# Shared 4 KB places for raw weights and raw x, and another order of score copies, in a gated mix of Fourier mixing and SwiGLU on one Trainium2 core

## The chip, the cores and the metric

The kernel runs on 1 core of one Trainium2 chip. The metric is the device time of one execution in microseconds (us). The time before is 725.82 us, the median of 3 runs (725.61 to 725.87).

## The reference, cut to what matters

For x of 2048 tokens by 512, all in float32:

```python
g = sigmoid((x * gate_w).sum(-1, keepdims=True))
a = dft_seq_re @ (x @ dft_hid_re.T) - dft_seq_im @ (x @ dft_hid_im.T)   # real part of the Fourier mix
b = (silu(x @ w1) * (x @ w3)) @ w2                                       # SwiGLU, inner width F = 1376
out = g * a + (1 - g) * b
```

## The kernel before, in words

**Products.** Every large product is done on blocks of 2 x 2 with seven products in place of eight (forms B11, B21, B22 and sums T1 to T4 of one side, and sums of the same kind of the other side). Each float32 operand is split into a rounded high part, made by ScalarE (`high`, L108, the activation at L109), and a remainder, made by VectorE (`low`, L111, the subtraction at L112). Each product then takes three matmuls (`mm3`, L118 and L120): high with high, high with low, low with high. A matmul has 128 x 128 stationary and 128 x 512 moving operands.

**Stage 1, gate and up (to about 220 us of the profile).** `ITEMS` lists 22 items (c, g): a chunk c of 128 of the F columns for the half g of the tokens (1024). Item 0 is done by `plain`; `gate_up(n)` does items 1 to 21. An item has seven products of six matmuls: X (five of them, one after another in one PSUM bank; `bank(n % 4)`), Y and Z. `first1` and `first2` of item n + LOOK (LOOK = 3) are done inside item n. The order inside an item is: X with form 4 and its read (L353), Z with form 5 and its read (L356), the next items' `first1`, X with form 3 and an addition on VectorE (L364), Z with form 2 and VectorE's L369 and L370, `first2` with an addition (L289), a copy of the score if there is one, and a Silu (L291), and last X with form 6 and the second half's Silu (L382), which frees the bank for the X of item n + 4, and VectorE's L383.

Raw weights of gate and up come in tiles `ws` of 128 x 1024 float32, 4 KB a partition, in a pool of their own with LOOK + 1 = 4 buffers (`load_w`). They are used for forms `wa` (rounded in the same item) and `wb` (sums `wu` on VectorE, then split). For the first 9 chunks `wb` is stored to DRAM and read back for the second half of the tokens (`load_wb`, L227).

The last chunk has 96 columns of F, and gate_w in the 32 that are left, so rows 96 to 127 of its bank are the scores of the output gate. `put_score(n, j, gate)` copies these 32 rows for the tokens' half j into a tile `sc`: for j = 0 on ScalarE from `s1`, for j = 1 on VectorE from the bank itself, ahead of the Silu of L382. Two small DMAs take them to `gs` in DRAM. It happens for items 11 and 12.

**Stage 2 (from about 220 us).** `STEPS` lists the work of eight blocks. Blocks F (four) multiply the sequence DFT (`cc`) with forms A1 and A2 of x; each has 7 forms x 4 quarters q = 28 steps of 12 matmuls. Blocks H (two) multiply what `hsp` holds of silu(gate) * up with forms of w2. Blocks Y (two) apply the hidden DFT to the F blocks' results, add H's and write out. In the order of a block: P1 (steps 0 to 3, form B11), P5 (4 to 7, T1), P6 (8 to 11, T2), P3 (12 to 15, B22), P7 (16 to 19, T3), P2 (20 to 23, B21), P4 (24 to 27, T4).

Every step ends with `advance(m)`: it issues loads of raw operands (`load_c`, on SP's queue), does a sum on VectorE (`sum_c`) for step m + 4, and splits the operand of step m + 3 (`split_c`) into one of four places `zo`. In the first block T3 is made by a DMA of POOL's queue that adds B12 to B22 in place (L651).

**Places.** `F4` is a list of 4 KB places (`wide` takes the first, `free` appends). In stage 1 it has 4 places (`f4_0` to `f4_3`, pool `f4_a`); when the pools of stage 1 are closed, 9 more are put ahead of them (`f4_4` to `f4_12`, pool `f4_b`), in memory that stage 1 used. Raw w2, raw x for the first forms (A1, `load_a`), the score tile and all raw operands of stage 2 take their places there. `load_c(0)` and `load_c(1)` are called at the ends of items 19 and 20, all else after stage 1.

**Around the first block.** `load_score(0)` reads the scores of the first half from `gs`, spread to all partitions, into a tile of the pool `ut`; it is issued right after stage 1, ahead of the loads of `advance(-1)`. `gates(0)` (ahead of step 2) does the sigmoid and stores g and 1 - g, up to signs, to DRAM; `load_gate` reads them back at step 8. The second forms A2 of x are made from x once more: `load_a2(p)` reads raw x (eight tiles of 128 x 1024) into one of two tiles of `ut` in turn (tags `u3`, `c21`), two ahead of step 4 and each later one when `make_a2(p - 2)` has been issued; `make_a2(p)` is issued ahead of step 8 + p and does one subtraction (L169) and two splits.

Each engine and each queue works in the order of the program, and waits there for semaphores. SP's queue carries nearly all loads, POOL's the stores to DRAM and the adding loads.

Of the kernel before, what the change touches and what calls it, by code (L numbers as in the profile page):

```python
# [7 lines left out]
F32 = mybir.dt.float32  # L8
F32R = mybir.dt.float32r
AF = mybir.ActivationFunctionType  # L10
ALU = mybir.AluOpType

P = 128
S = 2048
D = 512
F = 1376
# [5 lines left out]
NG = NST // 2  # L22
# [3 lines left out]
LOOK = 3  # L26
# [6 lines left out]
def fnet_swiglu_gate_kernel(  # L33
# [20 lines left out]
    nc = tc.nc  # L54

    def pool(name, bufs, side, space=None):
        kw = {} if space is None else {"space": space}
        cm = tc.tile_pool(name=name, bufs=bufs, side=side, reuse_waits="tile", **kw)
        return cm, cm.__enter__()
# [8 lines left out]
    zo_a_cm, zo_a = pool("zo_a", 1, "left")  # L68
    xo0_cm, xo0 = pool("xo0", 1, "left")
    f4_a_cm, f4_a = pool("f4_a", 1, "right")  # L70
    ws_cm, wsp = pool("ws", LOOK + 1, "right")
    wu_cm, wup = pool("wu", 1, "right")
    s1_cm, s1p = pool("s1", LOOK + 1, "right")
    wa_cm, wap = pool("wa", LOOK + 1, "right")
    wb_cm, wbp = pool("wb", 2, "right")
    u4_cm, u4p = pool("u4", 1, "right")
    h_cm, hp = pool("h", 2, "right")
    xo1_cm, xo1 = pool("xo1", 1, "right")
    gate_pools = (ws_cm, wu_cm, s1_cm, wa_cm, wb_cm, u4_cm, h_cm, xo1_cm)

    def bank(k, name):
        return psum.tile([P, 512], F32, tag=f"ps{k}", name=name)
# [3 lines left out]
    F4 = [(f4_a, f"f4_{k}") for k in range(4)]  # L86
# [10 lines left out]
    def wide(name):  # L97
        return take(F4, [P, 1024], F32, name)
# [4 lines left out]
    def free(*tiles):  # L103
        for t in tiles:
            _, places, at = HELD.pop(id(t))
            places.append(at)
# [28 lines left out]
    def flat(ap):  # L135
        return ap.rearrange("p a n -> p (a n)")
# [29 lines left out]
    def forms2(r, t2):  # L166

        r = r.rearrange("p (a n) -> p a n", a=4)
        nc.vector.tensor_sub(r[:, 0], r[:, 1], r[:, 0])  # L169
        split(flat(t2[:, 0, 0:2]), flat(t2[:, 1, 0:2]), flat(r[:, 2:4]))  # L170
        split(t2[:, 0, 2], t2[:, 1, 2], r[:, 0])
# [8 lines left out]
    NI = len(ITEMS)  # L180
# [22 lines left out]
    def sum_xo(g, k, t):  # L203
        ST[g, k] = t
        nc.vector.tensor_sub(t, *(ST[g, v] for v in SUMS[k]))  # L205
# [5 lines left out]
    def split_xo(g, k):  # L211
        split(*xo_parts(g, k))

    WS, WA, WB = {}, {}, {}
# [3 lines left out]

    def load_w(w, lo=0, hi=4):
        if lo == 0:  # L220
            WS[w] = wsp.tile([P, 4, 256], F32, tag="ws", name=f"ws{w}")
        nc.sync.dma_start(WS[w][:, lo:hi].rearrange("p a n -> p (a n)"),
                          w13[SETS[w], :, lo * 256 : hi * 256])

# [41 lines left out]
    def prod(ps, n, wi, xi, start, chain=False):  # L266
        w = WSET[n]
        w, wi = (WA[w], wi) if wi < 3 else (WB[w], wi - 3)
        x = XO[ITEMS[n][1]]
        for q in range(2):  # L270
            sl = slice(q * P, (q + 1) * P)
            mm3(ps, w[:, 0, wi, sl], w[:, 1, wi, sl], x[:, 0, xi, q, :], x[:, 1, xi, q, :],
                start and q == 0, q == 1, chain)
# [10 lines left out]
    def first2(n):  # L284

        y = bank(4 + n % 2, f"Y{n}")
        prod(y, n, 1, 1, True)
        s1 = G[n][1]
        nc.vector.tensor_add(s1, s1, y)  # L289
        put_score(n, 0, s1)  # L290
        nc.scalar.activation(s1, s1, AF.Silu)  # L291

    SC = {}

    def put_score(n, j, gate):


        c, g = ITEMS[n]
        if c < NC - 1:
            return  # L300
        if not SC:
            SC[0] = wide("sc")
        p = F % P - 32 * g
        t = SC[0].rearrange("p (b n) -> p b n", b=2)
        if j == 0:
            nc.scalar.activation(t[p : p + 32, j], gate[F % P :], AF.Copy)
        else:
            nc.vector.tensor_copy(t[p : p + 32, j], gate[F % P :])
        if j == 1:
            nc.gpsimd.dma_start(gs[2 * g : 2 * g + 2].rearrange("b o n -> o b n"), t[p : p + 1])  # L310
            if g == 1:
                at_end.setdefault(n + 1, []).append(lambda: free(SC[0]))
# [16 lines left out]
    def gate_up(n):  # L329
        last = NI - 1  # L330
        x, s1 = G.pop(n)
        z = bank(6 + n % 2, f"Z{n}")
        if n == last - 1:

            u2, g1 = (s1p.tile([P, 512], F32, tag="s1", name=f"{k}_{n}") for k in ("u2", "g1"))
        else:
            h = hp.tile([P, 1024], F32, tag="h", name=f"h{n}")
            u2, g1 = h[:, :512], h[:, 512:]
        u4 = u4p.tile([P, 512], F32, tag="u4", name=f"u4_{n}")
        nw = WSET[n + 1] if n < last else 0  # L340
        if nw in WB or nw == 0:
            nw = None
        elif back(nw):
            load_wb(nw)
            nw = None
        wa = WSET[n + LOOK + 1] if n + LOOK < last else 0
        if wa in WA or wa == 0:
            wa = None
        else:
            load_w(wa, 0, 3 if back(wa) else 4)  # L350

        prod(x, n, 4, 4, False, True)
        nc.scalar.activation(u2, x, AF.Copy)  # L353
        run(early, n)
        prod(z, n, 5, 5, True, True)
        nc.scalar.activation(u4, z, AF.Copy)  # L356
        if nw is not None:
            sums_wb(nw)
        if n + LOOK <= last:
            first1(n + LOOK)  # L360
        if nw is not None:
            high_wb(nw)
        prod(x, n, 3, 3, False, True)
        nc.vector.tensor_add(u4, u4, x)  # L364
        if nw is not None:
            low_wb(nw)
        run(mid, n)
        prod(z, n, 2, 6, False, True)
        nc.vector.tensor_add(u2, u2, z)  # L369
        nc.vector.tensor_mul(u2, s1, u2)  # L370
        store_h(n, 0, u2)
        if wa is not None:
            WA[wa] = wap.tile([P, 2, 3, 256], F32R, tag="wa", name=f"wa{wa}")
            parts_a = wa_parts(wa, 0, 3)
            high(parts_a[0], parts_a[2])
        if n + LOOK <= last:
            first2(n + LOOK)
        if wa is not None:
            low(*parts_a)
        prod(x, n, 6, 2, False, True)  # L380
        put_score(n, 1, x)
        nc.scalar.activation(g1, x, AF.Silu)  # L382
        nc.vector.tensor_mul(g1, g1, u4)  # L383
        store_h(n, 1, g1)
        run(at_end, n)
# [75 lines left out]
    prep_wa(1)  # L461
    first1(1)
    first2(1)
    sum_xo(0, "T1", hp.tile([P, 1024], F32, tag="h", name="t1"))
    sum_xo(0, "T2", ST[0, "B11"])
    prep_wa(2)
    first1(2)
    first2(2)
    split_xo(0, "T2")
    prep_wb(1)  # L470
    sum_xo(0, "T3", ST[0, "B12"])
# [1 line left out]
    prep_wa(3)  # L473
    first1(3)
    first2(3)
    split_xo(0, "T1")
    prep_wa(4)
    sum_xo(0, "T4", ST[0, "B21"])
# [3 lines left out]
    def do(work, n, f, *a):  # L482
        work.setdefault(n, []).append(lambda: f(*a))
# [64 lines left out]
    for n in range(NI):  # L548
# [6 lines left out]
        if n in A1_AT:  # L555
# [2 lines left out]
            do(early, n, lambda p=p: sums1_here(XR[p]))  # L558
            do(mid, n, high_a, p)
            do(early, n + 1, low_a, p)  # L560
    do(at_end, NI - 3, lambda: load_c(0))
    do(at_end, NI - 2, load_a, NG - 1)
    do(at_end, NI - 2, lambda: load_c(1))
    do(early, NI - 1, lambda: sums1_here(XR[NG - 1]))
    do(mid, NI - 1, lambda: split_c(0))
    do(at_end, NI - 1, lambda: split_c(1))
# [87 lines left out]
    def load_c(m):  # L654
        while LOADS and LOADS[0][0] <= m and F4:
            _, blk, k, q = LOADS.pop(0)
            r = RAW[blk, k, q] = wide(f"{k}_{blk}_{q}")
            n = cols(blk, q, k)
            nc.sync.dma_start(r[:, :n], block(blk, k, q)[:, :n])

    def advance(m):
        load_c(m + LEAD + AHEAD)
        sum_c(m + LEAD + 1)
        split_c(m + LEAD)
# [10 lines left out]
    f4_b_cm, f4_b = pool("f4_b", 1, "right")  # L675
    a2_cm, a2 = pool("a2", 1, "right")
    ut_cm, ut = pool("ut", 1, "right")
    F4[:0] = [(f4_b, f"f4_{k}") for k in range(4, 13)]
    ZO[:0] = [(zo_b, f"zo_{k}") for k in range(2, 4)]
    def load_a2(p):  # L680

        XR[p] = flat(ut.tile([P, 2, 512], F32, tag=("u3", "c21")[p % 2], name=f"xs{p}"))
        nc.sync.dma_start(XR[p], xn[p])

    def make_a2(p):
        A2.append(a2.tile([P, 2, 3, 256], F32R, tag=f"a2_{p}", name=f"a2_{p}"))
        forms2(XR.pop(p), A2[p])
        if p + 2 < NG:
            load_a2(p + 2)

    GATES = {}

    def load_score(g):
        t, ng = GATES[g] = [flat(ut.tile([P, 2, 512], F32, tag=k, name=f"{k}g{g}"))
                            for k in ("p5", "u2")]
        nc.sync.dma_start(t.rearrange("p (b n) -> p b n", b=2),
                          gs[2 * g : 2 * g + 2].rearrange("b o n -> o b n").to_broadcast([P, 2, 512]))

    load_score(0)
    high_a(NG - 1)  # L700
    low_a(NG - 1)
    advance(-1)

    def gates(g):

# [168 lines left out]
    def at(blk, n, f, *a):  # L874
        todo.setdefault(START[blk] + n, []).append((f, a))

    at(0, 4, load_a2, 0)
    at(0, 4, load_a2, 1)
    at(1, 1, load_score, 1)
    for p in range(NG):  # L880
        at(0, 8 + p, make_a2, p)
    at(0, 2, gates, 0)
    at(1, 3, gates, 1)
    late = [(w2, w2sp, p) for p in range(len(W2_AT), NP2)] + [(dd, dsp, p) for p in range(KD)]
    for i, (src, sp, p) in enumerate(late):
# [86 lines left out]
```

## Time and profile before

| | |
|---|---|
| median of 3 runs | 725.82 us (725.61 to 725.87) |
| profiled execution, its own time | 725.82 us |
| its span, first to last instruction | 724.0 us |
| TensorE, matmuls | 712.1 us busy (98%), 3089 matmuls |
| TensorE, weight loads | 582.2 us (80%) |
| VectorE | 603.3 us (83%), 731 instructions |
| ScalarE | 368.0 us (51%), 475 instructions |
| GpSimd | 67.6 us (9%) |
| mean granted clock of TensorE | 0.990 |
| DMA | 174.64 MB, mean 241 GB/s |

The engines are named PE (matmuls of TensorE), PEld (its weight loads), DVE (VectorE), ACT (ScalarE), POOL (GpSimd) and SPq (SP's queue of DMAs). Times in the profile are counted from the first instruction of the profiled execution. The busy share is a mean over stages; where an engine ends the wait of another, the waits and the chain of waits tell.

### The profile page before, as it was taken

To read this page: it belongs to the slowest core of one execution; us is meant where nothing else is said; L and a number is where in the kernel's file an instruction comes from. 1 tells how busy PE (TensorE), PEld (TensorE's weight loads), DVE (VectorE), ACT (ScalarE), POOL (GpSimd) and SP (SyncE) were. 2 spreads that over 40 slices of the span, in tenths; PEclk is the share of its full clock that TensorE was granted. 3 is DMA by queue.
4 is the path that set the end of the run, shared out by engine and by line. 5 is a ranking of instruction groups with operands and counts; after the bars stand their busy time and mean duration, and the time that the engine had idled before them with its cause. 6 is when DMAs were issued, how large, how long until landed. Compare 5 with 4: busy or idle time off the path is not lost.

```text
span 724.0 us, 8583 instructions
## 1 busy us (share of the span) xinstructions
PE 712.1 (98%) x3089; PEld 582.2 (80%) x3089; DVE 603.3 (83%) x731; ACT 368.0 (51%) x475; POOL 67.6 (9%) x122
## 2 busy tenths in 40 slices
PE   9999999999998999999999999999999999999997
PEld 6888888788886877888888888888888888888886
DVE  6988888887676968895999699987998797797985
ACT  6565465455444645455536444554545545445451
POOL 0011111121010010000011001100110010010000
PEclk9999999999998998999999999999999999999999
DMA  7575556589887499832289127915799962763932
GB/s 275 202 282 214 198 191 258 200 293 349 329 318 277 196 247 340 294 156 86 69 323 371 42 84 273 399 69 204 306 421 418 395 240 108 291 244 151 331 118 87
DMA packets 45979, 174.64 MB, mean 241 GB/s; under 512 B 5360, under 2 KB 5488, under 8 KB 42096
## 3 DMA queue, kind: packets, MB, share of 16 engines
q1 hardware_dynamic: 32464, 118.50, 44.6%
q0 software_dynamic: 13184, 55.07, 20.1%
q8 instruction: 24, 0.39, 0.2%
q10 hardware_dynamic: 288, 0.52, 0.2%
q14 instruction: 19, 0.16, 0.1%
HBM read 116.92 MB, written 57.16 MB: 240 GB/s over the span
## 4 chain that ended last, share of the span: by engine, by line
PE 88%; DVE 5%; DMA 3%; ACT 2%; issue 1%; SPq 0%; ACTq 0%; DVEq 0%
PE P L120 62%; PE X L120 14%; PE Z L120 7%; PE Y L120 4%; DVE zo L112 2%; DMA xs<-xn 1%; DMA B<-cc 1%; PE C L120 1%; DVE B L634 1%; ACT zo L109 1%; DMA xs_B<-xt 1%; DVE xo L112 0%; ACT h L382 0%; DVE xs_B L205 0%; ACT wb L109 0%
## 5 line engine op out<-in xcount | busy, mean ns | idle before, releaser
L120 PE MATMUL P<-zo,a 128*128 128x512 f32 x1344 | 312.4, 395 | 5.4 <-ACT zo L109 4.3
L120 PEld LDWEIGHTS P<-zo,a 128*128 128x128 f32 x1344 | 255.6, 191 | 62.0 <-ACT zo L109 5.1
L109 ACT ACTIVATE zo<-B 128x1024 fp32r<-128x1024 f32 (+1 forms) x182 | 189.1, 1044 | 184.3 <-PE P L120 95.3
L112 DVE TENSOR_TENSOR zo<-B,zo 128x1024 fp32r<-128x1024 f32 (+1 forms) x182 | 217.4, 1202 | 54.9 <-ACT zo L109 54.3
L120 PE MATMUL P<-zo,H 128*128 128x512 f32 x468 | 106.2, 389 | 0.0
L120 PEld LDWEIGHTS P<-zo,H 128*128 128x128 f32 x468 | 87.9, 188 | 18.2
L634 DVE TENSOR_TENSOR B<-B,B 128x1024 f32<-128x1024 f32 (+1 forms) x78 | 92.7, 1189 | 1.7 <-DMA B<-cc 1.6
L120 PE MATMUL X<-xo,wb 128*128 128x512 f32 x378 | 92.8, 389 | 0.0
L120 PEld LDWEIGHTS X<-xo,wb 128*128 128x128 f32 x378 | 70.9, 188 | 15.0 <-DVE u L364 0.3
L120 PE MATMUL P<-zo,Y 128*128 128x512 f32 x336 | 76.3, 389 | 0.0
L120 PEld LDWEIGHTS P<-zo,Y 128*128 128x128 f32 x336 | 63.1, 188 | 13.1
L319 POOL DMA_DIRECT2D hsp<-h x42 | 23.0, 548 | 127.6 <-DVE h L370 70.4
L120 PE MATMUL X<-xo,wa 128*128 128x512 f32 x126 | 32.6, 391 | 1.4 <-ACT h L382 1.4
L120 PE MATMUL Z<-xo,wa 128*128 128x512 f32 x126 | 32.3, 390 | 0.0
L120 PE MATMUL Y<-xo,wa 128*128 128x512 f32 x126 | 32.1, 389 | 0.0
L120 PE MATMUL Z<-xo,wb 128*128 128x512 f32 x126 | 32.1, 389 | 0.0
L120 PEld LDWEIGHTS X<-xo,wa 128*128 128x128 f32 x126 | 23.5, 188 | 7.1 <-ACT h L382 2.3
L847 ACT ACTIVATE zu<-P 128x512 f32<-128x512 f32 x32 | 19.0, 597 | 19.5 <-PE P L120 19.5
L120 PEld LDWEIGHTS Z<-xo,wa 128*128 128x128 f32 x126 | 23.6, 188 | 5.3 <-DVE xo L112 0.4
L120 PEld LDWEIGHTS Y<-xo,wa 128*128 128x128 f32 x126 | 23.6, 188 | 4.9
L120 PEld LDWEIGHTS Z<-xo,wb 128*128 128x128 f32 x126 | 23.6, 188 | 4.9
L637 DVE TENSOR_TENSOR B<-B,B 128x1024 f32<-128x1024 f32 x22 | 26.8, 1218 | 0.0
(134 smaller groups left out, 546.0 us busy)
## 6 DMA issues: line engine op xcount, KB each, us to landing
B<-cc SPq DMA_DIRECT2D x64, 512.0 KB, 7.0
hsp<-h POOLq DMA_DIRECT2D x42, 256.0 KB, 3.7
B<-hsp SPq DMA_DIRECT2D x20, 512.0 KB, 10.4
wbsp<-wb POOLq DMA_DIRECT2D x8, 1024.0 KB, 4.4
wb<-wbsp SPq DMA_DIRECT2D x8, 1024.0 KB, 6.3
B<-zsp SPq DMA_DIRECT2D x16, 512.0 KB, 8.1
H<-w2sp SPq DMA_DIRECT2D x6, 1024.0 KB, 9.3
ws<-w SPq DMA_DIRECT2D x11, 512.0 KB, 6.8
```

The lines of the kernel that those rows point to most:

```text
L109: nc.scalar.activation(hi, src, AF.Copy)
L112: nc.vector.tensor_sub(lo, src, hi.bitcast(F32))
L120: nc.tensor.matmul(ps, u, v, start=first and n == 0, stop=last and n == 2, skip_group_check=chain)
L319: nc.gpsimd.dma_start(hsp[g, b + k, j // 2, :, j % 2 * 512 : (j % 2 + 1) * 512], h)
L634: nc.vector.tensor_add(t, t, RAW[blk, b, q][:, :n])
L637: nc.vector.tensor_sub(t, RAW[blk, "B12", q], t)
L847: nc.scalar.activation(U[name][:, r], ps[r], AF.Copy)
```

## The change

Raw gate/up weights no longer have a pool of their own: `load_w` takes four further tags of `f4_a`, `f4_4` to `f4_7`, in turn. At the end of item 17 these four join `F4`, and the pool made after stage 1 has only `f4_8` to `f4_12`; there are 13 places as before. `load_c(0)` to `load_c(4)` are called at the ends of items 17 to 21.

Raw x for the second forms takes places from `F4`; `load_a2(p)` is issued ahead of step 4 + p, and `make_a2(p)`, at its old step, frees the place.

The second Silu of an item on ScalarE comes ahead of the score's copy, and the copy is on ScalarE for both halves. The Silu of the first half (`gate1`) leaves `first2` and comes behind both; ahead of item 1 it follows `first2` as before.

`load_score(0)` comes behind `advance(-1)`, and `gates(0)` ahead of step 4 in place of step 2.

On TensorE and on POOL's queue the order of instructions is the same as before. VectorE has two copies fewer and ScalarE two more.

```diff
@@ pools
-    ws_cm, wsp = pool("ws", LOOK + 1, "right")
...
@@ load_w
-            WS[w] = wsp.tile([P, 4, 256], F32, tag="ws", name=f"ws{w}")
+            WS[w] = f4_a.tile([P, 4, 256], F32, tag=f"f4_{4 + w % (LOOK + 1)}", name=f"ws{w}")
@@ first2
         put_score(n, 0, s1)
-        nc.scalar.activation(s1, s1, AF.Silu)
+
+    def gate1(n):
+        nc.scalar.activation(G[n][1], G[n][1], AF.Silu)
@@ put_score
-        if j == 0:
-            nc.scalar.activation(t[p : p + 32, j], gate[F % P :], AF.Copy)
-        else:
-            nc.vector.tensor_copy(t[p : p + 32, j], gate[F % P :])
+        nc.scalar.activation(t[p : p + 32, j], gate[F % P :], AF.Copy)
@@ gate_up
         prod(x, n, 6, 2, False, True)
+        nc.scalar.activation(g1, x, AF.Silu)
         put_score(n, 1, x)
-        nc.scalar.activation(g1, x, AF.Silu)
+        if n + LOOK <= last:
+            gate1(n + LOOK)
@@ loads of the first block, ends of items
-    do(at_end, NI - 3, lambda: load_c(0))
+    n = NI - 1 - LOOK
+    do(at_end, n - 1, F4.extend, [(f4_a, f"f4_{k}") for k in range(4, 5 + LOOK)])
+    for k in range(LOOK + 2):
+        do(at_end, n - 1 + k, lambda k=k: load_c(k))
     do(at_end, NI - 2, load_a, NG - 1)
-    do(at_end, NI - 2, lambda: load_c(1))
@@ after stage 1
-    F4[:0] = [(f4_b, f"f4_{k}") for k in range(4, 13)]
+    F4[:0] = [(f4_b, f"f4_{k}") for k in range(5 + LOOK, 13)]
@@ load_a2, make_a2
-        XR[p] = flat(ut.tile([P, 2, 512], F32, tag=("u3", "c21")[p % 2], name=f"xs{p}"))
+        XR[p] = wide(f"xs{p}")
         nc.sync.dma_start(XR[p], xn[p])
...
-        forms2(XR.pop(p), A2[p])
-        if p + 2 < NG:
-            load_a2(p + 2)
+        forms2(XR[p], A2[p])
+        free(XR.pop(p))
...
-    load_score(0)
     high_a(NG - 1)
     low_a(NG - 1)
     advance(-1)
+    load_score(0)
@@ steps
-    at(0, 4, load_a2, 0)
-    at(0, 4, load_a2, 1)
     at(1, 1, load_score, 1)
     for p in range(NG):
+        at(0, 4 + p, load_a2, p)
         at(0, 8 + p, make_a2, p)
-    at(0, 2, gates, 0)
+    at(0, 4, gates, 0)
     at(1, 3, gates, 1)
```

More of the change, by code (lines that the diff above doesn't have):

```diff
@@ L78, in fnet_swiglu_gate_kernel @@
     xo1_cm, xo1 = pool("xo1", 1, "right")
-    gate_pools = (ws_cm, wu_cm, s1_cm, wa_cm, wb_cm, u4_cm, h_cm, xo1_cm)
+    gate_pools = (wu_cm, s1_cm, wa_cm, wb_cm, u4_cm, h_cm, xo1_cm)
     def bank(k, name):
@@ L463, in fnet_swiglu_gate_kernel @@
     first2(1)
+    gate1(1)
     sum_xo(0, "T1", hp.tile([P, 1024], F32, tag="h", name="t1"))
@@ L468, in fnet_swiglu_gate_kernel @@
     first2(2)
+    gate1(2)
     split_xo(0, "T2")
@@ L475, in fnet_swiglu_gate_kernel @@
     first2(3)
+    gate1(3)
     split_xo(0, "T1")
```

## The prediction

> **What bounds the kernel now.** I read the page first, then the waits of TensorE, its timeline, the windows around its gaps, and the chain of waits there. The page's busy times and the granted clock by slices:
>
> ```profile
> PE   9999999999998999999999999999999999999997
> ...
> PEclk9999999999998998999999999999999999999999
> ```
>
> TensorE is busy throughout (712.1 of 724.0 us), so only its gaps and its slow stretches can be won. Two slices (13 and 16 of 40) are below full clock. The waits of TensorE name what ended the gaps:
>
> ```profile
> PE P L120 <- ACT zo L109: 4.3, 2, 2.3
> PE X L120 <- ACT h L382: 1.4, 1, 1.4
> ```
>
> Its timeline (start, duration; in brackets the idle time before) shows where: at the start of the first block's third step, at its step 16, nowhere later.
>
> ```profile
> 220.16 5.89 PE L120 MATMUL P<-zo,a 128*128 128x512 f32 x24
> 227.99 0.66 PE L120 MATMUL P<-zo,a 128*128 128x512 f32 x1 [1.94 <-ACT zo L109]
> 229.25 40.85 PE L120 MATMUL P<-zo,a 128*128 128x512 f32 x167 [0.60 <-DVE zo L112]
> 272.41 0.70 PE L120 MATMUL P<-zo,a 128*128 128x512 f32 x1 [2.32 <-ACT zo L109]
> 273.67 56.49 PE L120 MATMUL P<-zo,a 128*128 128x512 f32 x236 [0.56 <-DVE zo L112]
> ```
>
> The windows (length, busy PE, PEld, DVE, ACT, POOL; then granted clock, DMA share, GB/s) show that each of these gaps is followed by half clock:
>
> ```profile
> 226.00:228.00 2.00, 0.07 (x2) 0.01 (x1) 0.03 (x1) 1.06 (x1) 0.00 (x0) 1.00 1.01 379
> ...
> 230.00:232.00 2.00, 2.00 (x7) 1.52 (x6) 1.22 (x2) 0.15 (x1) 0.00 (x0) 0.50 1.03 420
> ...
> 276.00:278.00 2.00, 2.00 (x6) 1.61 (x5) 1.04 (x2) 0.23 (x1) 0.00 (x0) 0.50 1.03 420
> ```
>
> The chain of waits tells what each gap waited for (first the short one, then the two long ones):
>
> ```profile
> 143.85 0.70 DVE sc L308
> 144.58 0.61 ACT h L382
> ```
>
> ```profile
> 220.35 0.33 SPq L696
> ...
> 221.67 9.08 DMA B<-cc
> ...
> 260.92 9.18 DMA xs<-xn
> ```
>
> So: the score copy on VectorE held back the Silu that frees a bank; the cc loads left SP's queue only after the score load at 220.35, which waits for the last gate/up product; and raw x of the second forms was loaded in two alternating places, one behind the other.
>
> **What the gaps cost.** Products follow each other every 0.2267 us (1.36 us for 6), a step of 12 takes 2.72. *Short gap:* 1.39; and 12 products at 95.73 took 3.06 instead of 2.72 behind the same L382, 0.34. Together 1.73. *First long gap:* product 26 of the block was due at 220.16 + 25 x 0.2267 = 225.83 and came at 229.25: 3.42. The 167 products from there took 40.85 instead of 166 x 0.2267 + 0.39 = 38.02: 2.83 of slow clock. Together 6.25. *Second:* due at 270.17, came at 273.67: 3.50; 236 products in 56.49 instead of 53.66: 2.83. Together 6.33. In all 14.31.
>
> The Trainium skill ("TensorE: Matmul & The Clock Gate", Part 1) lets the clock fall after an idle window of some 3.4 us and rise after a busy one as long. The trace disagrees: 1.94 + 0.60 us idle sufficed, and the slow stretch lasted about 6.8 us. By an estimate from the page's length, a slow stretch would cost half of 3.4, 1.7, and the forecast below would be 2 x 1.13 higher, 715.2.
>
> **The change, part by part.**
>
> *Score copies and Silu order (items of gate/up).* The copy from the bank moves from VectorE (0.70) to ScalarE behind the second Silu; the first half's copy on ScalarE shows its price, 0.63. The first half's Silu (L291), which waits for VectorE's addition, moves behind both. At the short gap the bank's product ended at 140.8 and ScalarE was free at 141.45: Silu to 142.05, copy to 142.7, bank due at 143.84. The gap goes. What now queues behind L291's wait is L353, the read of the next item's bank: there the addition ended at 142.95, so L291 to 143.6, L353 to 144.2; its waiter is the item's third product, due at 145.2. Slack 1.0, so I book nothing; the upper bound is a rival below. Gain 1.73 (bounds 1.4 and 1.8).
>
> *Raw weights into the shared places.* Same four-fold rotation, same 11 + 9 loads: nothing. But four places return to the pool at item 17, so SP's queue issues one cc load behind each item's weights and x: at about 183, 191, 201, 208. The loads of B12's quarters 1 to 3 wait for the last product of item 20 (213.4), B22's first for item 21's last use of wa (218.8), and the score load goes behind them. In SP's queue they stand behind wb loads and ahead of xr7 and of the next wb. wb19 took 5.8 us from 206.75 and was due at 213.36: 0.8 of slack, with the same bytes ahead of it as now. xr7 (landed 215.1, used 216.0) has 512 KB more ahead, about 1.2 us at 420 GB/s; VectorE idles 0.38 and 0.26 before the next uses, so at most 0.3 remains. Bounds 0 and 1.5, taken 0.
>
> *First block's start.* B11's third quarter is there long before; step 2 needs only ScalarE's rounding and VectorE's remainder, the latter free at 224.2 (its last work at 223.08 takes 1.14), done at 225.4, due at 225.83. The first long gap goes, 6.25.
>
> *Raw x in shared places.* Five of eight loads go out by about 234, as sums free B11's places; nothing waits for them before 246. The other three stand in SP's queue behind the gate load, which waits for the gate store: the gates move from step 2 to step 4, behind the two reads of the first result, so the copy ends at 237.0, the store (6.8) at 244. Then each load waits for second forms 0, 1, 2 (done about 247.5, 250.5, 253.5) and lands 3.2 to 9.2 later; they are due at 258, 261, 264. All have slack, 1.3 at the worst. The four adding loads on POOL's queue (5.9 to 9.0 to landing) start at 252, 255, 258 and 261, due at 262, 265, 268 and 270.8: covered, by 0.6 in the last case. The second gap goes, 6.33.
>
> *What is late next: VectorE.* In the old run it caught up during the gaps. Without them it has from 224.2 to prepare step 19: 18 remainders and 8 sums of 1.14 (29.6), the gates, and 8 second forms. Of these the timeline shows the cycle:
>
> ```profile
> 250.56 0.41 DVE L169 TENSOR_TENSOR xs<-xs 128x256 f32<-128x256 f32 x1
> 250.89 1.02 DVE L112 TENSOR_TENSOR a<-xs,a 128x512 fp32r<-128x512 f32 x2
> 252.41 1.23 DVE L112 TENSOR_TENSOR zo<-B,zo 128x1024 fp32r<-128x1024 f32 x1 [0.50 <-ACT zo L109]
> 253.55 0.42 DVE L169 TENSOR_TENSOR xs<-xs 128x256 f32<-128x256 f32 x1
> ```
>
> From 250.56 to 253.55 a step with second forms takes 2.99, more than TensorE's 2.72; beyond the remainder that is 8 x 1.85 = 14.8. Gates: ScalarE ends rounding for step 6 at 232.1, reads twice (1.2), loads its table (1.28) and does the sigmoid (1.07) to 235.7; VectorE idles 1.2, scales 0.67, idles 0.5 for ScalarE's copy and rounding: 2.4. The result at step 15's end (two additions, two gate products, 282.02 and 283.23 show 1.2 a pair): 2.4. Sum 49.2, so step 19's remainder is ready at 273.4 against 220.16 + 19 x 2.72 + 0.23 = 272.07. I take 1.4, spread over steps 16 to 19 in waits of 0.1 to 0.8, too short for the clock (1.39 at 143.84 left it at 1.00). Bounds 0 (sums of 1.14 are start to start; any wait could hide) and 3 (late adding loads, or 0.5 more in the gates).
>
> The Trainium skill ("ScalarE: Activation LUTs", What ACT_TABLE_LOAD costs) adds a drain of about 1.38 us to the 1.28 of a table load. The trace shows none: the load starts 0.02 after the activation before it and the next starts 0.01 after it. By the page the time would be 1.4 higher, 714.3.
>
> **Sum.** 724.0 - 1.73 - 6.25 - 6.33 + 1.4 = 711.1 of span. The profiled execution took 725.82, 1.82 beyond its span and equal to the median of the runs, so 712.9.
>
> **Rivals.**
> *The moved wait costs more than it frees (slower).* Before, ScalarE waited 25.1 us in 14 waits at L291 for VectorE; now these waits stand ahead of L353. It decides once VectorE's addition ends over 2.7 us after the bank's product (then L353 misses the third product); the late ones I found ended 2.15 (142.95 against 140.8) and 1.87 later. If all 14 turned into waits of TensorE: 712.9 + 25.1 = 738.0; 12.9 of them make it slower than before. 4%.
> *The second gap stays, shorter:* the last x loads, behind the gate load and beside the adding loads, land 3 us late and the clock halves once: 712.9 + 3 + 2.83 = 718.7. For it, DMA share 1.0 from 260 to 286; against, the slack above. 7%.
> *The small waits trip the clock:* steps 16 to 19 hold 1.4 us of idle in 11 us. If that halves it once, 712.9 + 2.83 = 715.7. For it, 1.94 sufficed; against, 1.39 in one piece did not. 7%. The Trainium skill ("TensorE: Matmul & The Clock Gate", A second HAM failure mode) describes such an oscillation from micro-idling between groups.
> *The early loads don't help:* they stand behind wb loads in one queue, and the first gap stays: 712.9 + 6.25 = 719.2. Against, the times at which places free. 3%.
>
> **How the numbers follow.** My forecast, 712.9, has 79%; its own range is 710.8 (no VectorE lag, some tenths of other short waits gone) to 715. The range runs to 717.5, which takes in the clock rival. Left out are the stayed gaps and the slower case, 14%. A measurement here tells 0.2% (1.45 us) from no change. Every case but the first rival is faster: 0.95; the rest of that one mostly slower, 0.04, same 0.01.
>
> **What would show it.** Right: no full-clock loss after 220 in the granted clock (all slices 9, mean near 1.00); no wait of X for L382; waits of P for VectorE's zo at about 262 to 272 summing to 1 to 2; the xs loads issued at about 224 to 254. Wrong: any idle of 2 us at TensorE with 0.50 behind it; L353 or L356 in TensorE's waits during gate/up.

## The result, and the profile after

The changed kernel took 714.15 us (median of 4 runs, 712.96 to 715.32) beside 725.72 us (725.54 to 725.87) for the kernel before on the same chip: a ratio of 0.9841, 95% interval 0.9818 to 0.9863. The forecast was 712.9, with 710.8 to 717.5 around it. The four runs lie in two groups, 712.96 and 713.02, and 715.29 and 715.32; the profiled execution is one of the upper ones (715.29, span 713.5). Most of what follows asks what sets the quick and the late ones apart, since the forecast has one time. (Nine more runs of the same kernel, below, lie from 712.4 to 716.25, some between these values: it is a spread, not two fixed times.)

The page of the changed kernel, TensorE's busy tenths and its granted clock by slices:

```profile
PE   9999999999999999999999999999999999999997
...
PEclk9999999999999999999999999999999999999999
```

The two slices below full clock are gone. TensorE is busy for 706.0 of 713.5 us, before for 712.1 of 724.0: the 6.1 us fewer of work are nearly all the matmuls that ran at half clock (2 x 2.83), the rest of the gain is idle time. The windows that showed half clock before (length, busy PE, PEld, DVE, ACT, POOL; granted clock, DMA share, GB/s), now:

```profile
230.00:232.00 2.00, 2.00 (x11) 1.65 (x10) 2.00 (x2) 0.80 (x1) 0.00 (x0) 1.00 1.03 416
...
276.00:278.00 2.00, 2.00 (x10) 1.66 (x9) 1.89 (x3) 1.24 (x3) 0.00 (x0) 1.00 1.03 422
```

The waits of TensorE (us in all, times, longest) no longer name L382's `h` or ScalarE's `zo`. A new one stands in their place:

```profile
PE X L119 <- DMA wb<-wbsp: 1.3, 2, 0.8
...
PE P L119 <- DVE zo L111: 0.8, 1, 0.8
```

TensorE's timeline (start, duration; in brackets the idle time before) shows both:

```profile
205.29 1.67 PE L119 MATMUL X<-xo,wb 128*128 128x512 f32 x6 [0.54 <-DMA wb<-wbsp]
213.18 1.66 PE L119 MATMUL X<-xo,wb 128*128 128x512 f32 x6 [0.75 <-DMA wb<-wbsp]
220.13 53.20 PE L119 MATMUL P<-zo,a 128*128 128x512 f32 x229
274.09 46.08 PE L119 MATMUL P<-zo,a 128*128 128x512 f32 x202 [0.75 <-DVE zo L111]
```

The first block now runs from 220.13 to step 19 without a long gap. But it starts when it did before (220.16), though the short gap, which is gone, lies ahead of it. The two waits for `wb` account for most of that. Six products take 1.36, so the first X of item 20 was due 0.70 earlier than 205.29, and that of item 21 0.91 earlier than 213.18; the products right behind each wait lose another 0.15 or so: 1.9 in all. Step 19 was due at 220.13 + 19 x 2.72 + 0.23 = 272.04 and came at 274.09, 2.05 late. So 724.0 - 14.31 + 1.9 + 2.05 = 713.6, against a span of 713.5. That the two agree so well hides two smaller errors: the short gap was worth more than its 1.73 (see the account below), and in this profile the first product on `wa` comes 0.27 later than before.

The chain of waits (start, us, what) tells what each of the two waited for:

```profile
204.78 8.35 DMA wb<-wbsp
...
261.56 10.05 DMA B<-cc
...
271.71 1.07 ACT zo L108
...
272.81 1.24 DVE zo L111
```

The load of `wb` for item 21 took 8.35 us (5.8 in the profile before); the adding load of step 19's operand took 10.05, where the prediction had at most 9.0.

### The profile page after: what moved, and what is told of

It is laid out like the page before. It is cut to its first block, busy times and chain, and to the rows that moved or that the text cites. A ratio compares the mean times of both kernels' runs of the same rounds, so it can differ in the third digit from the quotient of the medians.

```text
span 713.5 us, 8596 instructions
## 1 busy us (share of the span) xinstructions
PE 706.0 (99%) x3089; PEld 578.5 (81%) x3089; DVE 600.8 (84%) x729; ACT 369.6 (52%) x477; POOL 67.5 (9%) x122
## 4 chain that ended last, share of the span: by engine, by line
PE 89%; issue 4%; DMA 4%; DVE 0%; ACT 0%; POOL 0%; SPq 0%; POOLq 0%; ACTq 0%
PE P L119 61%; PE X L119 15%; PE Z L119 8%; PE Y L119 4%; DMA B<-cc 1%; DMA wb<-wbsp 1%; PE C L119 1%; DMA p5g<-gs 1%; DMA xs_B<-xt 1%; DVE zo L111 0%; DVE xo L111 0%; ACT zo L108 0%; ACT xo L108 0%; POOL B L656 0%; SPq L221 0%
## 5 line engine op out<-in xcount | busy, mean ns | idle before, releaser
L119 PE MATMUL P<-zo,a 128*128 128x512 f32 x1344 | 306.5, 390 | 0.8 <-DVE zo L111 0.8
L119 PEld LDWEIGHTS P<-zo,a 128*128 128x128 f32 x1344 | 251.8, 188 | 55.5 <-DVE zo L111 3.4
L362 DVE TENSOR_TENSOR u<-u,X 128x512 f32<-128x512 f32 x21 | 14.4, 687 | 19.2 <-PE X L119 16.8
L379 ACT ACTIVATE h<-X 128x512 f32<-128x512 f32 x20 | 12.0, 598 | 30.8 <-PE X L119 30.6
```

Source lines behind the costliest of these rows:

```text
L119: nc.tensor.matmul(ps, u, v, start=first and n == 0, stop=last and n == 2, skip_group_check=chain)
```

## The experiments

Three groups: the changed kernel again and two edits for the waits for `wb` (with a third for VectorE's lag), then parts of the change undone, last the edits that had helped put together. Each group ran on one chip beside the kernel before. "Due" is worked out as above, at 2.72 us a step.

**The changed kernel once more.** No edit.

> The changed kernel once more, for what sets its two groups of times (713.0 and 715.3 us). Theory A: its wb loads of items 20 and 21 come late beside the early cc loads (in the profile of 715.3 they landed 7.3 and 8.3 us after issue against 5.5 and 5.8 before, and TensorE lost 0.70 and 0.91 us to them), and runs of 713.0 are those where they come in time. Then a profile near 713.0 shows no wait of X for wb, one near 715.3 shows about 1.3 us of it. Theory B: the wb waits are the same in both and the 2.3 us lie in the first block: then steps 16 to 19 differ by 2 us between the two.

Measured: 713.35 us (712.88, 712.88, 713.83, 714.76) beside 725.84, ratio 0.9832 (0.9818 to 0.9845). TensorE's timeline in the profiled execution, one of 712.88:

```profile
218.01 53.08 PE L119 MATMUL P<-zo,a 128*128 128x512 f32 x229
271.65 58.56 PE L119 MATMUL P<-zo,a 128*128 128x512 f32 x257 [0.56 <-DVE zo L111]
```

No product waits for `wb`: its last two loads landed after 6.5 and 6.3 us (7.3 and 8.3 in the profile above), and the first block starts at 218.01, 2.1 earlier. Same program, same order, nearly the same lag at step 19 (271.65 against 269.92, 1.73). So of the 2.4 us between the two spans, 1.9 is the landing of `wb`, 0.3 the lag, and 0.2 an earlier first product.

**`wb` in three loads, in the order of need.**

```diff
-        nc.sync.dma_start(WB[w].bitcast(F32), wbsp[SETS[w]])
+        for v in (slice(1, 3), slice(0, 1), slice(3, 4)):
+            nc.sync.dma_start(WB[w][:, :, v].bitcast(F32), wbsp[SETS[w]][:, :, v])
```

> The changed kernel, with each wb read back in three loads (forms 1 and 2 of wb first, as they are used, then form 0, then form 3) in place of one. Theory A (late wb loads cost 1.6 us in some runs): the half that the item's first product needs lands about 1.2 us sooner, the waits of X for wb go, and all runs lie in one group near 713.0 or a little lower (712.5 to 713.3). Theory B (the first block sets the groups): two groups at 713.0 and 715.3 remain. Upper bound: three issues in place of one cost SP 0.8 us more an item, which nothing waits for.

Measured: 714.59 us (714.31 to 714.78), ratio 0.9845 (0.9832 to 0.9859). One group of runs and no wait for `wb`, but no gain. TensorE's waits show what came instead, VectorE's addition for the last item's X:

```profile
PE X L119 <- DVE u L363: 0.7, 1, 0.7
```

The three loads take 1.84 to 1.88 us to issue on SP's queue (one takes 0.33), and the last `xr` behind them landed at 215.52 (214.38 in the profile without a wait); VectorE's sums that wait for it come ahead of that addition. The first block starts at 219.03. A miss: the wait moved to the next in the queue.

**The first block's `cc` loads later.** The first two only behind items 19 and 20, as in the kernel before; the others right behind.

```diff
-    for k in range(LOOK + 2):
-        do(at_end, n - 1 + k, lambda k=k: load_c(k))
+    do(at_end, NI - 3, lambda: load_c(0))
     do(at_end, NI - 2, load_a, NG - 1)
+    do(at_end, NI - 2, lambda: load_c(1))
```

> The changed kernel, with the four places joined to the pool at item 17 as now, but only one cc load issued behind items 19 and 20 each (as in the kernel before); all other cc loads follow in SP's queue right behind these, ahead of the score load. Theory A1 (what is in flight ahead of a wb load delays it): wb of items 20 and 21 land in about 5.5 and 5.8 us again, no wait for wb, 713.0 in all runs; the first block's third quarter is still there in time, so the first long gap stays away. Theory A2 (what is queued behind delays it too, because the 16 engines share all open transfers): the wb of item 21 now has five or more cc loads right behind it and takes 8 us or more, so its wait of 0.75 us stays; 713.5 to 715.3. Rival: the first long gap returns in part, since B11's quarters 2 and 3 land after 223: 716 or more with half clock behind it.

Measured: 713.08 us (712.59, 712.92, 713.25, 713.48), ratio 0.9825 (0.9811 to 0.9838). `wb` landed after 5.3 and 5.9 us, nothing waits for it, the first block starts at 217.79, and the first long gap stays away. So the loads issued ahead of `wb` delay it: without the early ones it lands as in the kernel before (5.5 and 5.8), with `xr` and one `cc` load right behind it as there. What more loads behind it would cost is not shown, since the other `cc` loads were issued only from 211.19 on, after its landing at 210.24. Nor is any load ahead of item 19 needed for the gap. B11's third quarter goes out at 211.19 here and, by the order of `F4`, into a place of the pool made after stage 1, not into one of the four of item 17; before, it stood behind the score load until 220.73. So in this run it is the score load's move that lets the quarter go early enough.

**The sigmoid's table early.** A sigmoid of 24 columns ahead of step 1, whose result nobody uses, loads the table; ScalarE's copy of the gates and their stores come one step later.

```diff
+        at(0 if g == 0 else 1, 5 if g == 0 else 4, gates_out, g, t, ng)
+
+    def gates_out(g, t, ng):
...
+    def early_table():
+        nc.scalar.activation(act0, act0, AF.Sigmoid)
...
+    at(0, 1, early_table)
```

> The changed kernel, with the sigmoid's table loaded by a 24-column activation ahead of step 1 (ScalarE idles 1.9 us there) and ScalarE's copy and the two stores of the gates one step later. Theory V (VectorE's lag at steps 16 to 19 costs about 2 us, 1.7 of it from VectorE's idle time at the gates): those idle times of 1.15 and 0.58 us go, and the time falls by 1.3 to 1.8 us within each group (711.4 and 713.7). Rival W (the adding load of quarter 3, which landed at 271.7, holds step 19): the fall is under 0.5 us.

Measured: 713.2 us (711.57, 712.91, 713.2, 713.47, 713.89), ratio 0.9829 (0.9815 to 0.9842). The profiled execution is the one of 711.57; its timeline of TensorE has the whole block in one row:

```profile
217.95 112.30 PE L119 MATMUL P<-zo,a 128*128 128x512 f32 x492
```

492 products at 0.2267 us are 491 x 0.2267 + 0.39 = 111.70, so at most 0.6 is lost where the changed kernel lost 1.73. VectorE reaches the second forms at 241.98, in the changed kernel's second profile at 243.94. VectorE's two waits at the gates (1.15 and 0.57) are gone. So the lag builds up around the gates, as the prediction had it, and 1.3 of it goes when the table load and ScalarE's copy are moved; the run does not part the two. The median moves by 0.15 only, and the runs lie 2.3 us apart. The early `cc` loads are still ahead of `wb`, which would account for it, but no slower run of this kernel has a profile.

**Raw x in two alternating tiles again.**

```diff
-        XR[p] = wide(f"xs{p}")
+        XR[p] = flat(ut.tile([P, 2, 512], F32, tag=("u3", "c21")[p % 2], name=f"xs{p}"))
...
-        forms2(XR[p], A2[p])
-        free(XR.pop(p))
+        forms2(XR.pop(p), A2[p])
+        if p + 2 < NG:
+            load_a2(p + 2)
...
+    at(0, 4, load_a2, 0)
+    at(0, 4, load_a2, 1)
...
-        at(0, 4 + p, load_a2, p)
```

> The changed kernel with raw x for the second forms in two alternating tiles again (each load issued two forms ahead), all else as changed. Theory: the second long gap comes back, since the loads of forms 5 to 7 wait for forms 3 to 5 (256.5, 259.5 and later) and land 6 to 9 us later: TensorE idles 3 to 5 us around steps 16 to 18 and runs at half clock behind it, plus 5 to 8 us in all, 718 to 721. Rival: the two gaps were one effect (the late cc loads made the x loads late), so with the first gone the loads are covered: under 715.

Measured: 720.34 us (719.38 to 721.97) beside 725.87, ratio 0.9926 (0.991 to 0.9943). TensorE's timeline shows a row of shorter waits in place of the one of 2.32 + 0.56:

```profile
264.86 0.51 PE L119 MATMUL P<-zo,a 128*128 128x512 f32 x1 [1.44 <-ACT zo L108]
266.12 7.70 PE L119 MATMUL P<-zo,a 128*128 128x512 f32 x24 [0.75 <-DVE zo L111]
274.59 2.99 PE L119 MATMUL P<-zo,a 128*128 128x512 f32 x12 [0.76 <-DVE zo L111]
```

and in its windows the clock falls, for a shorter time than before:

```profile
268.00:270.00 2.00, 2.00 (x6) 1.59 (x5) 1.55 (x3) 1.44 (x3) 0.00 (x0) 0.50 1.01 393
270.00:272.00 2.00, 1.96 (x8) 1.28 (x7) 1.13 (x2) 0.61 (x2) 0.00 (x0) 0.97 1.03 422
```

The expected time holds, its shape not quite. From 259.33 to 278.12 TensorE did 49 products, 11.1 us of work, in 18.8: 7.7 lost over four steps, of which the changed kernel loses 1.7 to 2.1 as well. The clock accounts for 1.7 of it: 0.68 from 266 to 268, 0.50 and then 0.97 make up about 3.4 us of half clock.

**Score copies and Silus as before.**

```diff
+        nc.scalar.activation(s1, s1, AF.Silu)
...
-        nc.scalar.activation(G[n][1], G[n][1], AF.Silu)
+        pass
...
-        nc.scalar.activation(t[p : p + 32, j], gate[F % P :], AF.Copy)
+        if j == 0:
+            nc.scalar.activation(t[p : p + 32, j], gate[F % P :], AF.Copy)
+        else:
+            nc.vector.tensor_copy(t[p : p + 32, j], gate[F % P :])
...
-        nc.scalar.activation(g1, x, AF.Silu)
         put_score(n, 1, x)
+        nc.scalar.activation(g1, x, AF.Silu)
```

> The changed kernel with the Silu of the first half in first2 again, the second half's score copy on VectorE ahead of the Silu. Theory: stage 1 is bound by TensorE behind that point, so the short gap at the score copy (1.4) and the 0.3 behind the late Silu come back in full: 714.5 to 715.2 against 712.9 to 713.4 of the changed kernel in its quicker runs; the wait of X for the second Silu shows 1.4 us. Rival: VectorE and the loads catch up during the gap (wb loads and xr loads then come in time, and VectorE's lag at step 19 shrinks), so half of it or more is given back: under 714.

Measured: 717.06 us (715.36, 716.0, 718.12, 718.31), ratio 0.9877 (0.9859 to 0.9896). TensorE's timeline in the profiled execution (718.12):

```profile
145.45 1.65 PE L119 MATMUL X<-xo,wa 128*128 128x512 f32 x6 [1.38 <-ACT h L384]
...
215.63 1.66 PE L119 MATMUL X<-xo,wb 128*128 128x512 f32 x6 [1.20 <-DMA wb<-wbsp]
```

The short gap is back with its 1.38 us, so it was rightly read. The time is above the expected 715.2, since the waits for `wb` are there too, 1.5 us in all. From start to start they cost 2.2. Stage 1, from its first X on `wa` to the first block, takes 201.95, against 197.5 in the profiles with neither, so some 2.3 of the 4.4 are left for the part.

**The score load ahead of the first block's loads again.**

```diff
+    load_score(0)
     advance(-1)
-    load_score(0)
```

> The changed kernel with the score load issued ahead of advance(-1) again, so that B12's quarters 1 to 3 and all of B22 wait in SP's queue for the last product of stage 1. Theory C (the early places end the first gap, the score load's place is not needed for it): B11 and B12's first quarter are there, the next is due at VectorE at 227.6 in the profile of 715.3 and lands before: within 0.5 us of the changed kernel, and wb of item 21 has 1 MB less behind it, so perhaps 0.5 lower (712.5 to 713.5). Rival D (the score load at the head was the gap): 716 or more, with a gap at steps 4 to 5 and half clock behind it.

Measured: 713.99 us (713.36, 713.57, 714.41, 716.01), ratio 0.9841 (0.9823 to 0.9859). No gap at the first block's third step; the profiled execution (714.41) has one wait for `wb`, 0.7 us, after landings of 7.5 and 7.6. So with the early loads the score load's move is not needed. With the move, the early loads were not needed either (`cc` loads later, above): each is enough, and the next kernel has neither.

**The early places undone.** The weights in their own pool again, the `cc` loads, the score load and the gates where they were; raw x in the shared places and the score part kept.

```diff
-            WS[w] = f4_a.tile([P, 4, 256], F32, tag=f"f4_{4 + w % (LOOK + 1)}", name=f"ws{w}")
+            WS[w] = wsp.tile([P, 4, 256], F32, tag="ws", name=f"ws{w}")
...
-    do(at_end, n - 1, F4.extend, [(f4_a, f"f4_{k}") for k in range(4, 5 + LOOK)])
-    for k in range(LOOK + 2):
-        do(at_end, n - 1 + k, lambda k=k: load_c(k))
+    do(at_end, NI - 3, lambda: load_c(0))
     do(at_end, NI - 2, load_a, NG - 1)
+    do(at_end, NI - 2, lambda: load_c(1))
...
+    load_score(0)
...
     advance(-1)
-    load_score(0)
...
-    at(0, 4, gates, 0)
+    at(0, 2, gates, 0)
```

> The kernel before with two parts of the change only: raw x in shared places, and the score copies and Silu order. Raw weights keep their own pool, cc loads, score load and gates stand as before. Theory: the first long gap stays with its half clock (6.25 us) and the other two go; the wb loads come in time, and VectorE catches up in the gap, so its lag of 1.9 at steps 16 to 19 goes too: 725.7 - 6.3 - 1.7 = 717.7 (717 to 718.5). Rival: the x loads, which now stand behind ten cc loads issued at once, come late and a second gap remains: 720 or more.

Measured: 717.88 us (717.66 to 718.24), ratio 0.9891 (0.9876 to 0.9905). The first gap is back, in TensorE's timeline,

```profile
226.28 0.80 PE L120 MATMUL P<-zo,a 128*128 128x512 f32 x1 [2.18 <-ACT zo L109]
227.53 49.07 PE L120 MATMUL P<-zo,a 128*128 128x512 f32 x204 [0.46 <-DVE zo L112]
```

with half clock behind it in the windows:

```profile
228.00:230.00 2.00, 2.00 (x6) 1.52 (x6) 1.06 (x1) 0.32 (x1) 0.00 (x0) 0.50 1.03 422
```

The block starts at 218.20, product 26 was due at 223.87 and came 3.66 late; the 204 products took 49.07 instead of 203 x 0.2267 + 0.39 = 46.41, 2.66 more. That is 6.32 for the gap, forecast at 6.25. The profiled execution is only 5.4 us longer than the changed kernel's without waits for `wb` (718.24 against 712.88), since in the gap VectorE catches up (step 19 is 0.6 late in place of 1.73). No early load stands ahead of `wb` (5.4 and 5.7 to landing, runs within 0.6).

**Both edits that helped, and the changed kernel beside them.** The later `cc` loads and the early table together, same diffs as above.

> The loads of raw gate and up weights start only behind items 19 and 20, and the sigmoid's table is loaded in an idle stretch of ScalarE with the copies and stores of the gates a step later. Theory: what is left of the shortfall is two terms that do not depend on each other, the late wb loads behind the cc loads (0 to 1.7 us, different from run to run) and VectorE's lag at step 19 (1.7 to 2.05 us, of which the early table takes away 1.3). Then every run should show no wait of a product for wb, a lag at step 19 of about 0.6 us or no wait of P at all, and a time of 711.2 to 712.2 us, with less than 1 us between its runs. Rival: the spread of the changed kernel is not from wb but from how a run happens to fall (HBM or the chip), and the two edits hide the same 1.3 us: then the time is about 713 us, as with either edit alone, and its runs lie 1 to 2 us apart.

> The changed kernel once more, beside the version with both edits on the same chip. Theory: 712.9 to 715.3 us, in the higher runs with waits of products for wb (loads 18 and 19 landing after 7 us and more), in the lower ones without; 1 to 2.5 us above the version with both edits. Rival: the same median as that version to within 0.5 us.

Measured: 711.47 us (711.0, 711.35, 711.6, 712.41) for the two edits, ratio 0.9801 (0.9787 to 0.9814); 713.24 us (712.4, 713.01, 713.24, 716.06, 716.25) for the changed kernel, ratio 0.984 (0.9819 to 0.9861); the kernel before took 726.08. It beats both kernels: 1.8 us below the changed one. Its spread of 1.4 is more than the expected 1, though less than the changed kernel's 3.9. In the profile nothing waits for `wb` (5.4 and 5.5 to landing), and the lag at step 19 is 1.0 instead of 0.6. The chain of waits names what sets it now:

```profile
257.82 10.87 DMA B<-cc
...
268.79 1.07 ACT zo L108
...
269.88 1.24 DVE zo L111
```

VectorE is early here, and the adding loads are late: it stands 1.36 us before step 18's remainder, whose adding load took 10.0 to landing, and 0.24 before step 19's, with 10.87. They are the next thing to move.

## Why the prediction was right, point by point

The time fell within its range, and the mechanisms of the gains and of the lag hold. The sizes of two terms do not (short gap, lag), and the reason for booking the early loads at nothing was wrong. In the profiled run of 712.88 (span 711.1, as forecast) the close agreement is partly luck: the short gap gave some 0.5 more than booked, the lag took 0.3 more, and 0.1 went to `wb`.

**Short gap, 1.73.** Right in mechanism, too small by 0.5. No product waits for the second Silu in any kernel with the new order, and the gap of 1.38 is back with the old one. From its first X on `wa` (20.37) to the first block (220.16) stage 1 took 199.79 before; in the six profiles with the new order in which neither a product nor a weight load waits for `wb` it takes 197.50 to 197.53. So 2.3 was freed. The sum took the idle time in brackets for the gap:

```profile
142.32 1.52 PE L120 MATMUL Z<-xo,wb 128*128 128x512 f32 x6
145.23 1.65 PE L120 MATMUL X<-xo,wa 128*128 128x512 f32 x6 [1.39 <-ACT h L382]
```

From start to start it is 2.91 - 1.36 = 1.55, and the products next to it lose another 0.16 and 0.13; the earlier stretch at 95.73 lost 0.39, not 0.34.

**First long gap, 6.25.** Right: away in every kernel that has the early loads or the later score load, and 6.32 in the one with neither. The prediction counted on both; in the runs either was enough, with the four places in the pool each time.

**Second long gap, 6.33.** Right in what it was put down to. With two alternating tiles the time rises to 720.34, 6 to 7 us above the changed kernel's medians. The loads of the shared places came as worked out: the last three are issued from 247.45, and the second forms never wait for them.

**VectorE's lag, 1.4.** Right in mechanism, too small by 0.3 to 0.7 (1.73 to 2.08 in three profiles of the changed kernel). VectorE's timeline in the profile after keeps to the forecast at the gates (1.2 and 0.5 of idle time were forecast):

```profile
235.63 0.76 DVE L714 TENSOR_SCALAR u2g<-p5g 128x512 f32<-128x512 f32 x2 [1.15 <-ACT p5g L711]
...
238.11 1.23 DVE L111 TENSOR_TENSOR zo<-B,zo 128x1024 fp32r<-128x1024 f32 x1 [0.58 <-ACT zo L108]
```

No single step of the sum failed. From the start of step 2's remainder (224.19, forecast 224.2) to the end of step 19's (274.03) VectorE took 49.8 in place of 49.2: 2.56 for the gates (2.4), 14.96 for the second forms (14.8), 2.67 for the result at step 15's end (2.4), and the last remainder runs 0.1 beyond its 1.14. The largest of these excesses comes from the last adding load, called "covered, by 0.6 in the last case". It took 10.05 where 9.0 was the longest row before and landed at 271.61, while the rounding would have had to start at about 271.5 to keep VectorE busy. That cost 0.18 here, and in the version with both edits it is the bound. In form the lag came as forecast: 0.75 of wait at step 19, and 1.1 of small ones before it (229 products took 53.20 instead of 228 x 0.2267 + 0.39 = 52.08); the clock stayed at 1.00.

**Early loads beside `wb`, booked at 0.** This is the step that was wrong, by 0 to 2.0 us in the three profiles of the changed kernel (start to start), where its bounds were 0 and 1.5. The reason given was that `wb` had "the same bytes ahead of it as now". That counted what SP's queue issues between one `wb` load and the next, and only for item 21. The load issued an item earlier was still on its way. SP's queue in the profile after, for item 20:

```profile
189.64 0.47 SPq L664 DMA_DIRECT2D B<-cc  x1
197.99 0.33 SPq L226 DMA_DIRECT2D wb<-wbsp  x1
```

That `cc` load took 9.5 to landing, so it landed 1.2 after `wb` was issued. Before, the last load ahead of item 20's `wb` (an `xr`) landed at 198.50, and `wb` was issued at 199.95. With `wb` late, `xr`, the `cc` load and the next `wb` behind it are pushed back too: item 21's `wb` was issued 3.6 ahead of the landing of the `cc` load before it, 2.0 in the profile before. Over the eleven profiles with whole `wb` loads the two go together. Where the load ahead lands at most 0.6 after item 20's `wb` is issued, or at most 2.1 after item 21's, `wb` takes 5.2 to 5.9; where it lands 0.9 to 1.6 (item 20) or 3.4 to 3.8 (item 21) after, it takes 6.3 to 7.5 and 7.6 to 8.6; in between (2.6 and 2.9, item 21) it takes 5.7 and 6.3. All seven sets of runs with the early loads ahead of whole `wb` loads lie 1.9 to 3.9 us apart, all four of other kernels 0.5 to 1.4. Why the loads ahead run later in some executions of the same program than in others stays open; that this parts the quick and the late runs is shown by profiles of both kinds, not for each run.

**The rivals.** The moved Silu: L351, the read that stands behind it, is in no wait of TensorE. The second gap, shorter: no. Small waits that trip the clock: no, a wait of 0.75 in one piece did not; the rival's condition was met in the kernel with two alternating tiles. Early loads that don't help: no, although the first block's start shows that they have a price.

**The rules of the Trainium skill.** By the Trainium skill's page "ScalarE: Activation LUTs", What ACT_TABLE_LOAD costs, the forecast would have been 714.3, near the median; but not for its reason. The table load in the profile after starts at 233.25, 0.02 after the read before it ends, takes 1.28, and the sigmoid starts at 234.54, 0.01 behind it: no drain.

By the Trainium skill ("TensorE: Matmul & The Clock Gate", Part 1) a slow stretch would cost 1.7 us, an estimate from its window of some 3.4 us. The kernel with two alternating tiles agrees (3.4 us of half clock, 1.7 lost). The kernel without the early places does not: behind 2.18 + 0.46 of idle time it lost 2.66, near the 2.83 of the trace before, which is the case that the forecast was about.

## What to carry to other kernels

A queue's load is delayed by what was issued before it and is still landing, also an item earlier: when transfers are moved ahead of a load with less than a microsecond of slack, price them by the landing times of its neighbours, not by the bytes between two issues. Runs that lie apart are worth a second profile: the same program showed in one what it hid in the other. Price a gap from start to start of its products, not by the idle time alone: here 0.5 of 2.3 us lay beside it. And when a gap closes, look for the engine that used to catch up in it; here its lag took back 1.7 to 2 us, and 1.3 of that went when a table load and a copy were moved out of VectorE's way.

## What the runs showed of the hardware that was not expected

- Half clock has more than one length. Idle times of 1.94 + 0.60 or 2.18 + 0.46 us, one product between, were followed by about 6.8 us of it (2.7 to 2.8 lost); 1.44 + 0.75, with 0.76 some 4 us ahead, by about 3.4 (1.7 lost); 1.38 alone, or 0.75 alone, by none.
- A `wb` load of 1 MB took 5.3 to 8.3 us to land in one profile of the changed kernel. For items 20 and 21 it followed how long the load ahead of it in SP's queue was still landing.
- The four adding loads of 512 KB of the first block took 5.9 to 9.0 us to landing in the profile before. The last of them took 8.5 there, 9.7 and 10.05 in two profiles of the changed kernel, and 10.87 with both edits, with a DMA share of 1.0 or more in all.
